# The planner's durations, hand-over times and gather latency as traced, and the slot tables built during the dense layers

## The chip, the cores and the metric

One core of a Trainium2 chip runs the program: TensorE (PE) multiplies, VectorE (DVE), ScalarE (ACT) and GpSimd (POOL) do the elementwise work, SyncE (SP) issues most DMAs. The metric is the device time of one execution in microseconds, the median of the runs shown. Each engine works through its instructions in the order in which they were emitted and waits on semaphores for the others.

## The reference, cut to what matters

```python
# attention: b=4, 8 heads, S=576, D=64
out_up    = repeat(softmax(scale * mean4(q) @ mean4(k).T) @ mean4(v), 4)      # downsampled by 4
out_local = softmax(where(|i - j| < 4, scale * q @ k.T, -1e9)) @ v            # local band
x = (out_up + out_local), as 2304 tokens x 512
# MoE 1: 8 experts, 512 -> 1024 -> 512, top 1
e_idx = argmax(x @ w_gate); gate_w = softmax(x @ w_gate)[e_idx]; eom = sigmoid(x @ w_output_gate)
out[mask_e] = gate_w * eom[:, e] * (relu(x[mask_e] @ w1[e]) @ w2[e])
# MoE 2, dense: 512 -> 2048 -> 512
h = relu(out @ w_in); result = (h * h) @ w_out
```

Everything is float32. The kernel multiplies each float32 pair as three products of rounded high and low parts (high x high, low x high, high x low).

## The kernel before, in words

Three parts follow one another on PE: attention for four batches (to about 165 us of the profile), the experts (165 to 433), the dense layers (433 to 848). The first two overlap on the other engines: weights of the first expert are split while the last batch is in attention.

**What sets the order.** No engine's order is written by hand. Class `Plan` holds operations, each with an engine, a duration in ns, a priority, what it depends on, and a ring of buffers that it takes. `Plan.order` is a greedy list scheduler over a modelled clock: it takes, again and again, the operation that could start first by that clock, and the priority breaks ties. The order in which operations are taken is the order in which they are emitted, and so the order on each engine. A duration that differs from the chip's costs nothing by itself: it moves operations in front of or behind others.

**Attention.** `reord` (L417) reorders q and k, PE transposes them, `tp_ev` (L437, ACT) evacuates them to kT and qT; `lc_k` (L584, L585, ACT) builds the block-diagonal kbd of the local band; `pd` (L508, ACT) is the exponential of the downsampled scores, `e` (L616, ACT) that of the local ones. POOL folds, VectorE does masks, maxima, sums and quotients.

**Routing and the first expert.** For the last batch the logits in PSUM (xp) go through a chain on VectorE, `mx` L696, `ex` L699, `eq` L702, `m` L705, `oh` L708, and on through counting (L713 to L828) to positions, tables of tokens and the ranking of the experts by size. The expert with most tokens of the first three batches gets a window of 256 tokens (rank -1) before the last batch is routed. Then eight windows of rank 0 to 7 follow, of 368 tokens down to 208.

**A window of an expert.** `gather` (L1121, POOL) issues an indirect DMA that fetches 128 rows of tokens into xg; `turn` (L1128, PE) transposes them into PSUM, `x_hi` (L1134, ACT) and `x_lo` (L1139, VectorE) split them into xh and xl. Weights come by DMA and are split: `w1h` L1153 and `w2h` L1160 on ACT, `w1l` L1156 on VectorE, `w2l` L1163 on POOL. Eight steps of `mm_h` (L1173, 12 matmuls into hp), `h_hi` (L1182, ACT), `h_lo` (L1187, VectorE, hl), `mm_y` (L1197, 12 matmuls into the four yp) follow; `yo` (L1204) takes the result out. The weights of the dense layers (64-bit words) are converted beside the experts (L1290 to L1301, `winl` L1216) and the early windows of the dense layers (`wol` L1391, POOL).

**The slot tables.** `compact_slots` and `overflow_slots` work out where each token's result goes, and `onehot_plan` turns slots into two tables, cid (for the main scatter, `tidc`) and oid (`tido`, for the rare tokens past a window), for each of four batches: `marks` builds a one-hot matrix oi_bm (L964), oi_a (L967) and oi_dg (L971, twice) on VectorE, `place` multiplies them on PE (L976, five short matmuls), `gather_up` adds the result (L983, L985). Some 30 us of small VectorE instructions in all. Before, cid may start when `mm_h` of rank 2 has come to its third step, oid at rank 4.

**Dense layers.** Six windows of 384 tokens, 16 steps each: `mm1` (L1347, 12 matmuls into hp, a ring of two), `relu` (L1352, ACT), `square` (L1355, VectorE, reads hp, which frees it), `s_hi` (L1359, ACT), `s_lo` (L1363, VectorE, hl), `mm2` (L1371, 9 matmuls, one step behind). At a window's end three `o_ev` and three `scatter` (POOL, indirect by tidc).

## Time and profile before

| | us |
|---|---|
| median of 3 runs | 850.5 (847.31 to 852.84) |
| profiled execution, its span | 848.5 |
| PE busy, share of the span | 786.0, 93% |
| VectorE busy, share | 497.0, 59% |
| ScalarE busy, share | 398.9, 47% |
| GpSimd busy, share | 254.8, 30% |

The profile is of one execution; 2.0 us lie between its span and the median. Busy time of PE is counted from overlapping matmuls, so 93% says where PE waits (the missing 7%), not how well it works. Shares are averages over parts with different limits: in attention ScalarE and VectorE work while PE has gaps, in the dense layers PE is never idle. The number of a line in the rows is that of the kernel before; after the change the same instruction stands one or two lines further down (L1139 becomes L1141, L964 becomes L966).

### The profile page before, as it was taken

What the parts mean: (1) busy time and instruction counts of PE and PEld (TensorE: products, weight loads), DVE (VectorE), ACT (ScalarE), POOL (GpSimd) and SP (SyncE); (2) the same over time, 40 slices, a digit from 0 to 9 for tenths busy, and PEclk for the clock granted to TensorE, in tenths of its full rate; (3) what the DMA queues carried; (4) which work ended last, traced back from release to release, by engine and by line L of the source; (5) the groups of instructions that cost most, each with busy time, mean ns of one, the idle gap of its engine ahead of it and who ended that gap; (6) DMA issues with size and microseconds to landing.
All of it is one profiled execution on the core that took longest, in us unless ns stands there. A gap on an engine that the chain in (4) does not pass through costs nothing.

```text
span 848.5 us, 15324 instructions
## 1 busy us (share of the span) xinstructions
PE 786.0 (93%) x5760; PEld 702.4 (83%) x5760; DVE 497.0 (59%) x1076; ACT 398.9 (47%) x753; POOL 254.8 (30%) x280
## 2 busy tenths in 40 slices
PE   4788998799989999898999999999999999999994
PEld 3655665598989889888998989999999999999994
DVE  6679999765547978987879973223222323322221
ACT  7998854555445456555645543223222322322221
POOL 5767543435434444445423330000001001001001
PEclk9999999899999999999999999999999999999998
DMA  8847487767467387668734332001100101001001
GB/s 224 219 112 201 131 242 221 241 221 234 153 204 231 129 256 231 178 196 258 244 121 153 120 100 68 9 1 38 38 0 38 39 1 38 1 0 38 1 1 40
DMA packets 102655, 105.39 MB, mean 124 GB/s; under 512 B 35356, under 2 KB 86556, under 8 KB 102576
## 3 DMA queue, kind: packets, MB, share of 16 engines
q1 hardware_dynamic: 99456, 94.41, 37.1%
q0 software_dynamic: 3120, 9.95, 3.4%
q8 instruction: 47, 0.77, 0.4%
q14 instruction: 32, 0.26, 0.1%
HBM read 84.95 MB, written 19.38 MB: 123 GB/s over the span
## 4 chain that ended last, share of the span: by engine, by line
PE 55%; DVE 19%; issue 10%; ACT 8%; DMA 5%; POOL 1%; SPq 0%; POOLq 0%; another core or an unknown queue 0%; ACTq 0%; DVEq 0%
PE hp L1347 18%; PE op L1371 18%; PE hp L1173 8%; PE yp L1197 8%; DMA xg<-xs_dram,idx 2%; DVE w1l L1156 2%; ACT kT L437 1%; DMA raw<-in_moe_w_in_dram 1%; ACT qT L437 1%; DVE f L1299 1%; DVE f L1301 1%; POOL w2l L1163 1%; ACT rr L417 1%; DVE f L1295 1%; DVE xT L668 1%
## 5 line engine op out<-in xcount | busy, mean ns | idle before, releaser
L1355 DVE SCALAR_TENSOR_TENSOR r<-hp,r 128x384 f32<-128x384 f32 x96 | 53.3, 555 | 191.9 <-ACT r L1352 191.9
L1352 ACT ACTIVATE r<-hp 128x384 f32<-128x384 f32 x96 | 47.1, 490 | 204.5 <-PE hp L1347 204.5
L1163 POOL TENSOR_TENSOR w2l<-r,w2h 128x512 fp32r<-128x512 f32 x72 | 101.8, 1423 | 134.6 <-ACT w2h L1160 134.1
L1347 PE MATMUL hp<-yh,winl 128*128 128x384 f32 x384 | 129.8, 338 | 0.0
L1347 PE MATMUL hp<-yh,winh 128*128 128x384 f32 x384 | 129.6, 338 | 0.0
L1347 PE MATMUL hp<-yl,winh 128*128 128x384 f32 x384 | 129.5, 337 | 0.0
L1371 PE MATMUL op<-woh,hl 128*128 128x512 f32 x288 | 113.9, 395 | 0.0
L1371 PE MATMUL op<-wol,hh 128*128 128x512 f32 x288 | 113.8, 395 | 0.1
L1381 POOL DMA_INDIRECT out_dram<-oo,tidc x18 | 17.3, 963 | 318.6 <-ACT oo L1378 315.0
L1371 PE MATMUL op<-woh,hh 128*128 128x512 f32 x288 | 112.9, 392 | 0.0
L1173 PE MATMUL hp<-xh,w1h 128*128 128x256 f32 (+7 forms) x288 | 88.6, 308 | 2.6 <-DVE hl L1187 2.6
L1173 PE MATMUL hp<-xl,w1h 128*128 128x256 f32 (+7 forms) x288 | 87.1, 302 | 0.0
L1173 PE MATMUL hp<-xh,w1l 128*128 128x256 f32 (+7 forms) x288 | 87.0, 302 | 0.0
L1197 PE MATMUL yp<-hl,w2h 128*128 128x368 f32 (+7 forms) x256 | 77.1, 301 | 3.0 <-DVE hl L1187 2.9
L1363 DVE TENSOR_TENSOR hl<-r,hh 128x384 fp32r<-128x384 f32 x96 | 53.9, 562 | 41.7 <-ACT hh L1359 41.7
L1197 PE MATMUL yp<-hh,w2h 128*128 128x368 f32 (+7 forms) x256 | 77.1, 301 | 0.9 <-DVE yo L1204 0.9
L1359 ACT ACTIVATE hh<-r 128x384 fp32r<-128x384 f32 x96 | 50.3, 524 | 54.7 <-DVE r L1355 49.7
L1197 PE MATMUL yp<-hh,w2l 128*128 128x368 f32 (+7 forms) x256 | 75.8, 296 | 0.0
L1347 PEld LDWEIGHTS hp<-yl,winh 128*128 128x128 f32 x384 | 72.3, 188 | 4.0
L1347 PEld LDWEIGHTS hp<-yh,winh 128*128 128x128 f32 x384 | 72.2, 188 | 3.7
L1347 PEld LDWEIGHTS hp<-yh,winl 128*128 128x128 f32 x384 | 72.1, 188 | 0.0
L1371 PEld LDWEIGHTS op<-woh,hl 128*128 128x128 f32 x288 | 54.1, 188 | 12.1 <-DVE hl L1363 0.3
(304 smaller groups left out, 1661.0 us busy)
## 6 DMA issues: line engine op xcount, KB each, us to landing
r<-in_moe_w_dram SPq DMA_DIRECT2D x72, 512.0 KB, 4.3
raw<-in_moe_w_in_dram SPq DMA_DIRECT2D x16, 512.0 KB, 4.7
raw<-in_moe_w_out_dram SPq DMA_DIRECT2D x16, 512.0 KB, 3.5
vbd<-in_v_dram SPq DMA_DIRECT2D x96, 64.0 KB, 3.1
yT_dram<-zero SPq DMA_DIRECT2D x8, 576.0 KB, 4.3
yr<-yT_dram SPq DMA_DIRECT2D x6, 768.0 KB, 5.2
...
```

Of the source, the lines that this page charges most:

```text
L437: self.nc.scalar.activation(dst, tp, AF.Copy)
L1156: nc.vector.tensor_tensor(W1[r, f][1], R1[r, f // 2][:, :, P * (f % 2):P * (f % 2) + P], W1[r, f][0].bitcast(F32), op=ALU.subtract)
L1163: nc.gpsimd.tensor_tensor(W2[r, f][1], R2[r, f // 2][:, f % 2, :], W2[r, f][0].bitcast(F32), op=ALU.subtract)
L1173: nc.tensor.matmul(out=ps[:, :cap], lhsT=a[:, k, :], rhs=b[:, k, :cap], start=(n == 0), stop=(n == 11))
L1197: nc.tensor.matmul(out=Y[r][c][:, :cap], lhsT=a[:, P * c:P * c + P], rhs=b[:, :cap], start=(f == 0 and n == 0), stop=(f == 7 and n == 2))
L1347: nc.tensor.matmul(out=ps[:, :WN], lhsT=a[:, k, :], rhs=b[:, k, :], start=(n == 0), stop=(n == 11))
L1352: nc.scalar.activation(r, PS[w, f][:, :WN], AF.Relu)
L1355: nc.vector.scalar_tensor_tensor(SQ[w, f], PS[w, f][:, :WN], 0.0, SQ[w, f], op0=ALU.max, op1=ALU.mult)
L1359: nc.scalar.activation(SQ[w, f, 1][0], SQ[w, f], AF.Copy)
L1363: nc.vector.tensor_tensor(sl, SQ[w, f], sh.bitcast(F32), op=ALU.subtract)
L1371: nc.tensor.matmul(out=O[w][t], lhsT=a[:, P * t:P * t + P], rhs=b, start=(f == 0 and n == 0), stop=(f == 15 and n == 2))
L1381: ins = nc.gpsimd.indirect_dma_start(out=self.out, out_offset=bass.IndirectOffsetOnAxis(ap=self.tidc[:, 3 * w + t:3 * w + t + 1], axis=0), ...
```

## The change

Three things, none of which changes what is computed. First, `Plan.order`'s model: a hand-over between engines was 230 ns for all, and is now 260 after PE, 150 after ACT, 125 after VectorE, 110 after POOL, 230 after SP, 40 more when POOL receives, 120 (was 130) on one engine; a DMA occupies the modelled queue 1.2 times as long. Second, durations in the model: `tp_ev` 490 to 880 and 270 to 310, `fold_end` 940 to 1500, `lc_k` 1520 to 1780, `lc_s` 1600 to 1400, `pv_mm` 1010 to 1090, `reord` 900 to 950, `mm_h` and `mm_y` from 5 ns a token and 20 to 5.43 ns a token, a gather 1050 to 1270 with its latency from 1900 to 4500, `x_hi` somewhat less, `w1_hi` and `w2_hi` 500 to 530, `w2_lo` 1220 to 1420, the conversions 500 to 575, 520 to 540 and 1240 to 1420, `mm1` 1930 to 2110, `mm2` 1930 to 2090, `scatter` 1050 to 1270. Third, the tables: cid depends on the first `mm1` of dense window 1, oid on that of window 2, both at a late priority; `place` takes its PSUM buffer from the ring of `mm1` (hp); the dense layers' pools (`sw2`) no longer wait for the tables. Docstrings go. The core of the diff:

```diff
@@ Plan.order
-        ops, gives, hop = self.ops, self.gives, 230
+        ops, gives = self.ops, self.gives
+        after = dict(PE=260, ACT=150, DVE=125, POOL=110, SP=230)
+        hop = lambda a, b: after.get(a, 230) + (40 if b == "POOL" else 0)
...
-                        early[o] = max([0] + [end[x] + (hop if ops[x]["eng"] != d["eng"] else 0 if d["eng"] in ("PE", "SP") else 130) if ops[x]["eng"] else start[x] for x in d["deps"]])
+                        early[o] = max([0] + [end[x] + (hop(ops[x]["eng"], d["eng"]) if ops[x]["eng"] != d["eng"] else 0 if d["eng"] in ("PE", "SP") else 120) if ops[x]["eng"] else start[x] for x in d["deps"]])
...
-                dma_free = max(dma_free, t + d["dur"]) + d["dma"]
+                dma_free = max(dma_free, t + d["dur"]) + 1.2 * d["dma"]
@@ onehot_plan
-            U["ps"] = self.qx.tile([P, 4, P], F32, name="xp").rearrange("p a b -> p (a b)")[:, 0:2 * ncol]
+            U["ps"] = self.qh.tile([P, 512], F32, name="hp")[:, 0:2 * ncol]
...
-            op(nm + "_p", (b,), "PE", 120, prio - 40, place, [(nm + "_m", b)], take="qx")
+            op(nm + "_p", (b,), "PE", 150, prio - 40, place, [(nm + "_m", b)], take="qh")
...
@@ moe1_plan
-            mm = 12 * cap / 2.4 + 20
+            mm = 12 * max(118, 0.4525 * cap)
...
-                op("gather", (r, k), "POOL", 1050, at(-5, -3), gather, early + [("fa_i",) if first else ("fr_i", min(r, 1))] + rows(r),
-                   lat=1900, dma=600, take="xg")
+                op("gather", (r, k), "POOL", 1270, at(-5, -3), gather, early + [("fa_i",) if first else ("fr_i", min(r, 1))] + rows(r),
+                   lat=4500, dma=600, take="xg")
...
-        op("cmp", (), "DVE", [80, 230, 230, 230, 230, 100, 100, 100, 100, 150], 60, self.compact_slots, [("sw1",), ("fr_o",), ("mm_h", 2, 2)])
-        self.onehot_plan("cid", lambda: self.cp, 18, lambda: self.tidc, 60, [("cmp",)])
-        op("ovs", (), "DVE", [240] * 24, 61, self.overflow_slots, [("cid_f",), ("mm_h", 4, 2)])
-        self.onehot_plan("oid", lambda: self.ov, NOV, lambda: self.tido, 61, [("ovs",)])
+        op("cmp", (), "DVE", [80, 230, 230, 230, 230, 100, 100, 100, 100, 150], 118, self.compact_slots, [("sw2",), ("fr_o",), ("mm1", 1, 0)])
+        self.onehot_plan("cid", lambda: self.cp, 18, lambda: self.tidc, 118, [("cmp",)])
+        op("ovs", (), "DVE", [240] * 24, 150, self.overflow_slots, [("cid_f",), ("mm1", 2, 0)])
+        self.onehot_plan("oid", lambda: self.ov, NOV, lambda: self.tido, 150, [("ovs",)])
@@ moe2_plan
-        op("sw2", (), None, 0, 200, moe2_pools, [o for o in one if o[0] in ("mm_h", "mm_y", "y_out", "y_st", "x_hi", "x_lo", "cid_p", "cid_f", "oid_p", "oid_f")] + [("sw2a",)])
+        op("sw2", (), None, 0, 200, moe2_pools, [o for o in one if o[0] in ("mm_h", "mm_y", "y_out", "y_st", "x_hi", "x_lo")] + [("sw2a",)])
...
-                op("mm1", (w, f), "PE", 1930, t, mm1, [("cxi", f)] + [("y_lo", w, k) for k in range(4)], take="qh")
+                op("mm1", (w, f), "PE", 2110, t, mm1, [("cxi", f)] + [("y_lo", w, k) for k in range(4)], take="qh")
```

Where it moves instructions, as the order of emission shows. PE, window of rank 1, before: the first `turn` (xp<-ident,xg) of rank 1 stands inside rank 0's window, behind 48 `mm_h` and the first 12 `mm_y` matmuls of rank 0 (yp; the x behind a row counts matmuls).

```order
L1197 MATMUL yp_3427<-hh,w2h 128x368
L1197 MATMUL yp_3427<-hl,w2h 128x368
L1197 MATMUL yp_3427<-hh,w2l 128x368
L1128 MATMUL xp<-ident,xg 128x128 x4
L1197 MATMUL yp_3424<-hh,w2h 128x368
```

PE, the same place after the change:

```order
L1199 MATMUL yp_3427<-hh,w2h 128x368
L1199 MATMUL yp_3427<-hl,w2h 128x368
L1199 MATMUL yp_3427<-hh,w2l 128x368
L1130 MATMUL xp<-ident,xg 128x128 x8
L1175 MATMUL hp<-xh,w1h 128x368
```

The turn stands behind the first 24 `mm_y` matmuls instead of 12, and its two full chunks are together. The first turn of rank 2 moves by 12 matmuls likewise, and its gather on POOL stands behind six w2l since rank 1's gathers, where it stood behind seven. The first turns of ranks 5 and 7 stand behind 36 `mm_y` matmuls of the window that runs, instead of 24; that of rank 4 keeps its place.

VectorE, the end of the last batch's routing, before (w1l: weights of the first expert; mx to oh: the routing chain; xl: the first expert's tokens, low part):

```order
L668 TENSOR_TENSOR xT<-tx,dso 128x4x96
L1156 TENSOR_TENSOR w1l<-r_2647,w1h 128x512 x2
L696 TENSOR_REDUCE mx<-xp 128x5
L699 TENSOR_TENSOR ex<-xp,mx 128x40
L702 SCALAR_TENSOR_TENSOR eq<-ex,w_87 128x40
L1139 TENSOR_TENSOR xl<-hp,xh 128x4x128
L705 TENSOR_REDUCE m_2811<-eq 128x5
L708 SCALAR_TENSOR_TENSOR oh<-m_2811,eq 128x40
L1139 TENSOR_TENSOR xl<-hp,xh 128x4x128
L831 TENSOR_TENSOR ot<-oh,tokhl 128x80
```

VectorE, the same place after the change, and further down the two xl:

```order
L670 TENSOR_TENSOR xT<-tx,dso 128x4x96
L1158 TENSOR_TENSOR w1l<-r_2641,w1h 128x512
L698 TENSOR_REDUCE mx<-xp 128x5
L701 TENSOR_TENSOR ex<-xp,mx 128x40
L704 SCALAR_TENSOR_TENSOR eq<-ex,w_87 128x40
L707 TENSOR_REDUCE m_2776<-eq 128x5
L710 SCALAR_TENSOR_TENSOR oh<-m_2776,eq 128x40
L833 TENSOR_TENSOR ot<-oh,tokhl 128x80
```

```order
L907 TENSOR_REDUCE offe<-gn 128x8
L828 TENSOR_TENSOR tok<-th,xp 128x40
L1141 TENSOR_TENSOR xl<-hp,xh 128x4x128
L924 TENSOR_TENSOR tokr<-tok 128x24
L909 TENSOR_TENSOR offe<-offe,ca 128x8
L926 TENSOR_TENSOR tokr<-tokr,ra 128x24
L911 TENSOR_TENSOR gn<-ro,offe 128x64
L928 TENSOR_TENSOR tokr<-tokr,tok 128x24
L915 TENSOR_REDUCE offi<-gn 128x8
L1141 TENSOR_TENSOR xl<-hp,xh 128x4x128
```

One w1l has gone from in front of the chain, and both xl have moved from within it to behind the routing's tables (30 and 37 rows after oh). On POOL in the same place five w2l in a row were emitted behind the two gathers of the first expert; after the change one w2l stands ahead of the gathers, then one w2l, xo, two w2l. On PE the second `turn` of the first expert now stands behind the five matmuls L820 (th, of the routing).

VectorE, the first table (cid), before, in the expert layer:

```order
L958 CAST oi_pf<-oi_pi 128x40
L964 TENSOR_TENSOR oi_bm<-iob,oi_pf 128x640
L1139 TENSOR_TENSOR xl<-xp,xh 128x4x32
L967 TENSOR_TENSOR oi_a_4351<-iob,oi_pf 128x90
L971 TENSOR_TENSOR oi_dg<-oi_a_4351,tokhl 128x5x18 x2
L1187 SCALAR_TENSOR_TENSOR hl<-hp,hh 128x312
L1156 TENSOR_TENSOR w1l<-r_4214,w1h 128x512
L983 COPY oi_acc<-xp 128x36
```

VectorE, the first table after the change, in window 1 of the dense layers (r: square, hl: s_lo):

```order
L1357 SCALAR_TENSOR_TENSOR r<-hp,r 128x384
L960 CAST oi_pf<-oi_pi 128x40
L966 TENSOR_TENSOR oi_bm<-iob,oi_pf 128x640
L1365 TENSOR_TENSOR hl<-r,hh 128x384
L969 TENSOR_TENSOR oi_a_7168<-iob,oi_pf 128x90
L973 TENSOR_TENSOR oi_dg<-oi_a_7168,tokhl 128x5x18 x2
L985 COPY oi_acc<-hp 128x36
L966 TENSOR_TENSOR oi_bm<-iob,oi_pf 128x640
L1357 SCALAR_TENSOR_TENSOR r<-hp,r 128x384
L969 TENSOR_TENSOR oi_a_7208<-iob,oi_pf 128x90
L973 TENSOR_TENSOR oi_dg<-oi_a_7208,tokhl 128x5x18 x2
```

The table's instructions of one batch stand between `square` and `s_lo` of a dense step instead of between `h_lo` and `w1l`; on PE the five matmuls of `place` stand between an `mm1` and an `mm2`, four times in window 1 and four times in window 2, and no longer between `mm_h` and `mm_y`.

## Rows read from the trace of the kernel before

**Rows 1.** Windows: stretch, length, busy of PE PEld DVE ACT POOL, clock, DMA.

```profile
18.50:40.00 21.50, 16.42 (x268) 13.01 (x272) 14.39 (x32) 21.36 (x29) 14.16 (x24) 1.00 0.78 199
...
165.40:433.00 267.60, 248.65 (x1851) 243.04 (x1848) 199.35 (x400) 143.66 (x287) 120.26 (x90) 0.98 0.66 208
...
466.00:836.00 370.00, 369.93 (x1848) 334.24 (x1847) 131.97 (x233) 110.06 (x219) 27.65 (x25) 1.00 0.09 31
```

**Rows 2.** Waits of PE in the expert layer, 165 to 433: total, times, longest.

```profile
PE xp L1128 <- DMA xg<-xs_dram,idx: 8.2, 6, 2.5
PE xp L976 <- DVE oi_dg L971: 4.3, 4, 1.4
PE xp L713 <- DVE oh L708: 3.7, 1, 3.7
PE yp L1197 <- DVE hl L1187: 2.9, 5, 1.2
PE hp L1173 <- DVE hl L1187: 2.6, 1, 2.6
```

**Rows 3.** Windows with PE's granted clock behind three stalls, columns as in rows 1.

```profile
165.40:171.20 5.80, 5.80 (x32) 5.63 (x29) 4.73 (x22) 1.86 (x5) 1.59 (x1) 0.50 0.87 311
...
236.70:239.90 3.20, 3.20 (x14) 3.20 (x13) 1.98 (x3) 0.60 (x1) 0.00 (x0) 0.55 0.63 186
...
359.50:363.70 4.20, 4.18 (x24) 4.18 (x24) 3.13 (x8) 0.63 (x1) 0.00 (x0) 0.65 0.92 194
```

**Rows 4.** Timeline before the first expert: start, duration, instruction, idle before.

```profile
157.59 6.07 DVE L1156 TENSOR_TENSOR w1l<-r,w1h 128x512 fp32r<-128x512 f32 x2 [0.43 <-ACT w1h L1153]
157.72 5.39 POOL L1163 TENSOR_TENSOR w2l<-r,w2h 128x512 fp32r<-128x512 f32 x4
...
165.23 0.19 PE L713 MATMUL xp<-oh,tri 128*128 128x40 bf16 x1 [3.71 <-DVE oh L708]
```

**Rows 5.** Timeline of VectorE behind oh, columns as in rows 4.

```profile
165.84 0.19 DVE L723 TENSOR_TENSOR zs<-xp,oh 128x40 f32<-128x40 f32 x1
...
167.23 0.82 DVE L806 TENSOR_TENSOR bm<-iob,pi 128x640 bf16<-128x640 f32 x1
167.96 1.26 DVE L773 TENSOR_SCALAR xo<-xo,s 128x512 f32<-128x512 f32 x1
...
169.57 0.56 DVE L813 TENSOR_TENSOR dg<-k,ot 128x400 bf16<-128x400 f32 x1
```

**Rows 6.** DMA issues of the page: gathers, count, median us to landing.

```profile
xg<-xs_dram,idx POOLq DMA_INDIRECT x21, 6.5
```

**Rows 7.** Instructions of VectorE by line, 260 to 390: count, busy, mean.

```profile
L1156 DVE TENSOR_TENSOR w1l<-r,w1h 128x512 fp32r<-128x512 f32 x35 | 25.0, 715 | 2.4 <-ACT w1h L1153 2.0
...
L964 DVE TENSOR_TENSOR oi_bm<-iob,oi_pf 128x640 bf16<-128x640 f32 x8 | 7.6, 955 | 0.1
...
L967 DVE TENSOR_TENSOR oi_a<-iob,oi_pf 128x90 f32<-128x90 f32 (+1 forms) x8 | 6.3, 792 | 0.0
```

**Rows 8.** Timeline at a stall of PE behind the second table.

```profile
359.05 0.42 DVE L1187 SCALAR_TENSOR_TENSOR hl<-hp,hh 128x256 fp32r<-128x256 f32 x1
...
359.52 0.58 PE L1173 MATMUL hp<-xh,w1h 128*128 128x256 f32 x1 [2.56 <-DVE hl L1187]
```

**Rows 9.** Timeline at a place of the first table, POOL idle since 281.88.

```profile
283.11 0.24 DVE L967 TENSOR_TENSOR oi_a<-iob,oi_pf 128x90 f32<-128x90 f32 x1
```

**Rows 10.** Instructions of ScalarE by line, 18.5 to 60.

```profile
L437 ACT ACTIVATE qT<-tp 128x512 f32<-128x512 f32 (+1 forms) x12 | 11.1, 1002 | 0.1
...
L616 ACT ACTIVATE e<-e 128x512 f32<-128x512 f32 x4 | 2.6, 658 | 0.0
```

**Rows 11.** Timeline of a dense step; its matmuls in the chain.

```profile
512.22 0.56 DVE L1363 TENSOR_TENSOR hl<-r,hh 128x384 fp32r<-128x384 f32 x1 [0.59 <-ACT hh L1359]
...
512.60 2.11 PE hp L1347 x12
514.71 2.09 PE op L1371 x9
```

More of the change, by code (lines that the diff above doesn't have):

```diff
@@ L109, in order @@
                     if len(hs) >= self.rings[d["take"]]:
-                        after = gives[hs[-self.rings[d["take"]]]]
-                        if any(x not in end for x in after):
+                        freed = gives[hs[-self.rings[d["take"]]]]
+                        if any(x not in end for x in freed):
                             continue
-                        t = max([t] + [end[x] + hop for x in after])
+                        t = max([t] + [end[x] + hop(ops[x]["eng"], d["eng"]) for x in freed])
                 c = (t, d["prio"], o)
@@ L283, in plan_b @@
             for i in range(2):
-                op("reord", (b, nm, i), "ACT", 900, tau - 0.2, self.reord, [("load", b, nm, i)], take="rr")
+                op("reord", (b, nm, i), "ACT", 950, tau - 0.2, self.reord, [("load", b, nm, i)], take="rr")
                 self.plan.give("raw", ("load", b, nm, i), ("reord", b, nm, i))
@@ L330, in plan_b @@
             i = (b, t3)
-            op("lc_k", i, "ACT", 1520, k - 0.2, self.lc_k, [("tp_ev", b, "k", t) for t in range(4 + (t3 == 2))], take="kbd")
-            op("lc_s", i, "PE", 1600, k, self.lc_s, [("lc_k",) + i] + [("tp_ev", b, "q", t) for t in range(4 + (t3 == 2))], take="psc")
+            op("lc_k", i, "ACT", 1780, k - 0.2, self.lc_k, [("tp_ev", b, "k", t) for t in range(4 + (t3 == 2))], take="kbd")
+            op("lc_s", i, "PE", 1400, k, self.lc_s, [("lc_k",) + i] + [("tp_ev", b, "q", t) for t in range(4 + (t3 == 2))], take="psc")
             self.plan.give("kbd", ("lc_k",) + i, ("lc_s",) + i)
@@ L1230, in plan_moe1 @@
                 n = min(P, cap - P * k)
-                op("gather", (r, k), "POOL", 1050, at(-5, -3), gather, early + [("fa_i",) if first else ("fr_i", min(r, 1))] + rows(r),
-                   lat=1900, dma=600, take="xg")
+                op("gather", (r, k), "POOL", 1270, at(-5, -3), gather, early + [("fa_i",) if first else ("fr_i", min(r, 1))] + rows(r),
+                   lat=4500, dma=600, take="xg")
                 op("turn", (r, k), "PE", 440, at(0, -6), turn, [("gather", r, k)], take="qh" if first else "qx")
                 give("xg", ("gather", r, k), ("turn", r, k))
-                op("x_hi", (r, k), "ACT", 3.8 * n + 20, at(0, -6), x_hi, [("turn", r, k)], take="x" if k == 0 else None)
+                op("x_hi", (r, k), "ACT", 3.55 * n + 30, at(0, -6), x_hi, [("turn", r, k)], take="x" if k == 0 else None)
                 op("x_lo", (r, k), "DVE", 4.2 * n + 70, at(0, -6), x_lo, [("x_hi", r, k)])
@@ L1243, in plan_moe1 @@
                 for f in (2 * s, 2 * s + 1):
[L1244 removed]
+                    op("w1_hi", (r, f), "ACT", 530, at(f, f - 4), w1_hi, [("load1", r, s)], take="w1")
                     op("w1_lo", (r, f), "DVE", 600, at(f, f - 3.5), w1_lo, [("w1_hi", r, f)])
[L1246 to L1247 removed]
+                    op("w2_hi", (r, f), "ACT", 530, at(f + 5, f - 3.9), w2_hi, [("load2", r, s)], take="w2")
+                    op("w2_lo", (r, f), "POOL", 1420, at(f + 5, f - 3.4), w2_lo, [("w2_hi", r, f)])
                     give("w1", ("w1_hi", r, f), ("mm_h", r, f))
@@ L1394, in plan_moe2 @@
         for f in range(16):
-            self.conv_plan("o", f, tau - 4 + 2 * f, [("sw2a",) if f < 5 else ("sw2",)], wo_hi, wo_lo, "POOL", 1240)
+            self.conv_plan("o", f, tau - 4 + 2 * f, [("sw2a",) if f < 5 else ("sw2",)], wo_hi, wo_lo, "POOL", 1420)
         for w in range(6):
@@ L1414, in plan_moe2 @@
                 give("rr2", ("relu", w, f), ("s_lo", w, f))
-                op("mm2", (w, f), "PE", 1930, t + 1, mm2, [("s_lo", w, f), ("cxo", f), ("sw2",), ("mm2", w, f - 1)], take="qo" if f == 0 else None)
+                op("mm2", (w, f), "PE", 2090, t + 1, mm2, [("s_lo", w, f), ("cxo", f), ("sw2",), ("mm2", w, f - 1)], take="qo" if f == 0 else None)
                 give("h", ("s_hi", w, f), ("mm2", w, f))
@@ L1418, in plan_moe2 @@
                 op("o_ev", (w, t), ("ACT", "DVE")[t % 2], 600, tau + 32, o_ev, [("mm2", w, 15)], take="oo")
-                op("scatter", (w, t), "POOL", 1050, tau + 32, scatter, [("o_ev", w, t), ("cid_f",), ("zero_y", 0)], lat=2200, dma=750)
+                op("scatter", (w, t), "POOL", 1270, tau + 32, scatter, [("o_ev", w, t), ("cid_f",), ("zero_y", 0)], lat=2200, dma=750)
                 give("oo", ("o_ev", w, t), ("scatter", w, t))
```

15 lines of the change are left out of this document (6 added, 9 removed).

## The prediction

> **What bounds the kernel now.** I read the windows first, then the waits of TensorE in the expert layer, then the timeline round each wait, and last the chain in a dense step.
>
> The windows split the span in three. In the dense layers PE is busy for 369.93 of 370.00 us [rows 1]: nothing to win there, only to lose. In the expert layer it is busy for 248.65 of 267.60 us, so 18.95 us are stalls. Attention is the third part: ScalarE is busy for 21.36 of 21.50 us from 18.5 to 40 us, VectorE for 14.39 only, which is to say that VectorE is fed late by ScalarE.
>
> The waits say what the stalls of the expert layer are [rows 2]: PE waits 8.2 us in 6 turns for a gather to land; 4.3 us in 4 places for a slot table (oi_dg); 2.9 and 2.6 us for hl, the low part that VectorE makes. The 3.7 us for oh lie just ahead of the first expert. The 2.6 us for hl belong to the second table too: its oi_bm and the rest stand in front of that hl on VectorE, and the first mm_h of the next step starts when it is done [rows 8].
>
> After a stall the clock counts again. Behind the waits at 236.0 and 359.5 the granted clock is 0.55 for 3.20 us and 0.65 for 4.20 us; behind the 3.7 us before the first expert it is 0.50 for 5.80 us [rows 3]. At the full clock the work of such a stretch would take its length times the clock, so these cost 3.20 x 0.45 = 1.4, 4.20 x 0.35 = 1.5 and 5.80 x 0.5 = 2.9 us.
>
> **The change, part by part.** The sum is made against the profiled execution's span, 848.5 us; the median of the runs shown is 2.0 us above it, and I add that at the end.
>
> *Gathers.* The model had a gather land 2.95 us after its issue began (1050 + 1900 ns); the median on the chip is 6.5 us [rows 6]. So turns were placed where the gather could not have landed. The new numbers make 5.77 us. The order shows the result: the first turns of ranks 1, 2, 3, 5 and 7 stand 12 matmuls, about 2 us, later behind the same gather, and rank 2's gather leaves POOL one w2l earlier. The longest wait was 2.5 us; 5 of the 6 waits should go, or nearly. What stays is 6.5 - 5.8 = 0.7 us at one or two of them, and rank 4, whose turn keeps its place. I take -7.2 of the 8.2.
>
> *Tables out of the expert layer.* The 4.3 us for oi_dg go with the five matmuls that waited. Of the 5.5 us for hl I take -4: the 2.6 are behind table work by the row [rows 8], and two of the shorter ones stand among the table's instructions. The matmuls of place move and cost as much there as here, so they are nil in the sum. Of the slow stretches behind stalls, 1.4 + 1.5 = -2.9. VectorE, no longer carrying some 30 us of table work between 268 and 385, must still serve w1l, hl, xl and the conversions; another order on all engines will put some new waits between 0 and 8 us there. I take +3, about what the hl and yo waits without tables and gathers come to now, and keep 0 and 8 as the ends.
>
> Expert layer: -7.2 - 4.3 - 4 - 2.9 + 3 = -15.4.
>
> *Start of the first expert.* Two w1l took 6.07 us on VectorE while four w2l ran on POOL for 5.39 us [rows 4]; a w1l takes 0.715 us on the mean [rows 7]. The new order has one w1l less in front of the chain of the last batch's routing, and on POOL a w2l, two gathers, a w2l and xo instead of five w2l in a row. Where two w1l took 6.07 us one will take 0.7, so oh should come some 5 us earlier, at 160.2 instead of 165.2. But the first expert does not start then. Its two xl have moved behind the routing's tables, and on PE its second turn stands behind th (L820), which needs bm and dg. From zs to bm 15 small instructions start in 1.4 us, 0.1 us each; bm takes 0.82, xo 1.26, dg 0.56 [rows 5]. To dg it is some 20 x 0.1 + 2 x 0.7 (w1l) + 0.8 + 1.2 + 0.6 = 6.0 us; then th 0.7, the turn 0.65, two hand-overs and x_hi some 1.0: 8.4 us. So the first mm_h starts near 168.6 instead of 165.4: **+3.2**, between 0 (if the instructions fit into waits) and +6 (if POOL still holds VectorE up, below). The stretch at clock 0.50 behind it stays, since PE still idles before it.
>
> *Tables in the dense layers.* A dense step takes 2.11 + 2.09 = 4.2 us of PE, and hl is done at 512.22 + 0.56 = 512.78, while the mm2 that needs it starts at 514.71: 1.9 us of slack [rows 11]. On VectorE a step needs two instructions of 0.56, 1.1 of 4.2 us, and the table adds up to one oi_bm, one oi_a and two oi_dg: by the rows of the expert layer some 0.95 + 0.8 + 0.7 = 2.4 us in each of 8 steps [rows 7], and less with POOL idle, where an oi_a took 0.24 us [rows 9]. In sum VectorE has 3.5 of 4.2 us to do. At worst all 2.4 us stand in the way of a step's square and hl, less what VectorE would have waited for s_hi anyway: hl is then 0.5 us past its slack. oi_bm in front of square also holds the hp of an mm1 longer, whose ring has two. I take **+0.5**, between 0 and +4 (8 steps late by 0.5).
>
> *Attention.* The order of ScalarE has two qT, a pair of kbd and two e fewer in front of the first exponential of batch 0's downsampled part. With 0.66 us for e and 1.0 for qT [rows 10] those six are 4 to 6 us that VectorE and PE get their first work earlier. But total work is unchanged, and what is put off comes later; VectorE's idle time from 18.5 to 40 is 21.5 - 14.39 = 7.1 us, the most that this could give. I take **-3**, between -8 and +4 (the same six instructions late where they matter).
>
> *Durations without a place of their own* (mm_h, mm1, conversions, scatter) only make the model's PE slower and nearer to the chip; POOL has 27.65 us of work in 370 [rows 1], so the scatter's is nothing. Where they shift something it is in the +3.
>
> Sum: -3 + 3.2 - 15.4 + 0.5 = -14.7, so a span of 833.8, and with the 2.0 us above it **836 us**.
>
> **The rivals.**
>
> *New waits eat the gain.* A list scheduler's order is brittle: the waits in the expert layer now come from five sources, and taking two away lets the next come up. For it: VectorE is busy for 199 of 267.6 us there [rows 1], 30 of it table work. Against: what is taken away is the longest of the waits, and 12 matmuls later is the direct answer to each. If new waits are 9 instead of 3 us, the time is 842; with attention at 0 as well, 845.
>
> *POOL holds VectorE up.* The row shows it now: w1l at 3.0 instead of 0.7 us beside w2l [rows 4]. If the w2l that stay in the new order fall on the routing chain, each instruction caught can lose most of a w2l, 5.39 / 4 = 1.35 us; two of them make the first expert start at +6 instead of +3.2: 839. [...]
>
> *Slower: the dense steps lose.* If the table work puts hl past its 1.9 us of slack, PE stalls in each step that carries it, and a stalled PE's clock falls besides. Some 14 steps carry table work. To end 1% above the median, 859, each would have to lose (859 - 836) / 14 = 1.6 us, that is hl 3.5 us late. For it: VectorE at 3.5 of 4.2 us. Against: 2.4 us of extra work a step cannot be 3.5 us late unless it runs longer than in the expert layer. The same side has attention at +4 and the first expert at +6 with no gain at the hl waits.
>
> *The moved tables do nothing.* The waits for oi_dg would be taken by hl waits; the gathers alone give -7.2 and the clock -1.4. With the other waits as they are, -3 + 3.2 - 7.2 - 1.4 + 0.5 = -7.9: 843.
>
> **How the numbers follow.** My forecast, all waits down to about a fifth: 0.57, with its own range 829 to 842. New waits eat the gain, or the tables give nothing (842 to 849): 0.25. POOL holds up VectorE (839, within the first range): counted in the 0.57. Attention and first expert both good, below 829: 0.10. Slower by the dense steps or attention: 0.08. The range 824 to 849 leaves out the last and some of the lowest. A change of about 1% is what a measurement of this kernel can tell from none: below 842 0.70, 842 to 859 0.22, above 859 0.08.
>
> **What would show it.** In the waits of PE in the expert layer the rows for xg and oi_dg gone or below 1.5 us together, and hl below 3. The windows: the expert layer 252 us long instead of 267.6, with PE above 97%. The first mm_h at 168 to 169 if attention gave nothing, 165 to 166 if it gave 3, behind an oh that is 5 us earlier. In the dense layers PE still above 99.5% busy, its steps in windows 1 and 2 at 4.2 to 4.4 us. Wrong if the first mm_h comes after 172, if new waits for w1l, w2l or yo sum to more than 5 us, or if PE waits for square or hl in the dense windows 1 and 2.

## The result: 1.0% slower, and the profile after

The changed kernel takes 856.9 us (855.4 to 858.1) against 849.3 us: ratio 1.0102, 95% interval 1.0059 to 1.0144. 836 was forecast, so the direction was wrong too. The profiled execution has a span of 855.8 us, 7.3 above that of before.

The windows of after, cut where its parts meet (stretch, length, busy of PE PEld DVE ACT POOL, clock, DMA), to be read beside [rows 1]:

```profile
18.50:40.00 21.50, 16.98 (x267) 13.15 (x267) 16.35 (x42) 20.44 (x28) 16.46 (x27) 1.00 0.85 210
...
166.80:175.50 8.70, 2.02 (x13) 1.31 (x11) 8.63 (x30) 2.41 (x4) 3.79 (x4) 0.50 0.77 246
175.50:433.00 257.50, 246.98 (x1812) 241.32 (x1813) 166.97 (x273) 142.11 (x284) 115.92 (x90) 0.98 0.66 211
433.00:466.00 33.00, 31.77 (x159) 27.62 (x158) 29.40 (x51) 17.68 (x36) 8.27 (x6) 1.00 0.47 149
466.00:843.30 377.30, 374.38 (x1898) 336.13 (x1897) 153.12 (x328) 110.24 (x221) 26.53 (x24) 1.00 0.09 29
```

VectorE does get its work earlier (16.35 instead of 14.39 us busy from 18.5 to 40). The expert layer is 10 us shorter, 257.5 instead of 267.6. But it begins 10 us later, at 175.5 instead of 165.4, after 8.7 us in which PE hardly works. And the dense layers, which had PE busy without a break, now have gaps.

PE's waits after, of three stretches (140 to 175, 175 to 433, 433 to the end), to be read beside [rows 2]:

```profile
PE xp L820 <- DVE dg L815: 6.0, 1, 6.0
PE hp L1130 <- DMA xg<-xs_dram,idxa: 2.3, 1, 2.3
...
PE xp L715 <- DVE oh L710: 0.8, 1, 0.8
```

```profile
PE yp L1199 <- DVE hl L1189: 2.9, 6, 0.8
PE xp L1130 <- DVE xl L1141: 2.2, 1, 2.2
PE yp L1199 <- ACT yo L1208: 2.0, 1, 2.0
PE yp L1199 <- ACT hh L1184: 1.0, 2, 0.6
PE xp L1130 <- DMA xg<-xs_dram,idx: 0.7, 2, 0.5
```

```profile
PE op L1373 <- DVE hl L1365: 2.3, 4, 1.3
PE op L1373 <- ACT hh L1361: 1.8, 4, 0.8
```

In the expert layer the waits for gathers (8.2 to 0.7) and for oi_dg (4.3 to none) are gone as forecast; waits for xl and hh are new, and that for yo is 2.0 instead of 0.9 us. The 3.7 us for oh have become 6.0 us for dg. The dense layers had no wait at all before; the 4.1 us here all lie in window 0, where no table work is.

Where the 7.3 us are, from five places of the two timelines (the start of the last xT and of oh on VectorE, the first mm_h, the first mm1, the end of PE's last matmul):

| | before | after | difference |
|---|---|---|---|
| last xT | 156.60 | 160.21 | +3.6 |
| last xT to oh | 8.38 | 3.18 | -5.2 |
| oh to first mm_h | 0.42 | 12.08 | +11.7 |
| expert layer, first mm_h to first mm1 | 267.68 | 257.61 | -10.1 |
| dense layers, first mm1 to end of PE | 404.74 | 411.46 | +6.7 |
| behind PE's end | 10.67 | 11.22 | +0.6 |

### The profile page after: what moved, and what is told of

It reads as the page before. It is cut to its first block, busy times and chain, and to the rows that moved or that the text cites. A ratio compares the mean times of both kernels' runs of the same rounds, so it can differ in the third digit from the quotient of the medians.

```text
span 855.8 us, 15327 instructions
## 1 busy us (share of the span) xinstructions
PE 794.0 (93%) x5760; PEld 702.2 (82%) x5760; DVE 490.9 (57%) x1076; ACT 399.5 (47%) x753; POOL 250.4 (29%) x280
## 4 chain that ended last, share of the span: by engine, by line
PE 59%; DVE 16%; issue 10%; ACT 7%; DMA 6%; POOL 1%; SPq 0%; POOLq 0%; another core or an unknown queue 0%; ACTq 0%; DVEq 0%
PE hp L1349 18%; PE op L1373 17%; PE yp L1199 10%; PE hp L1175 8%; DVE f L1301 2%; DVE f L1297 2%; DMA xg<-xs_dram,idx 2%; DMA raw<-in_moe_w_in_dram 1%; DVE f L1303 1%; PE tp L755 1%; DVE f L1299 1%; ACT rr L419 1%; PE po L650 1%; ACT f L1292 1%; ACT kT L439 1%
## 5 line engine op out<-in xcount | busy, mean ns | idle before, releaser
L1165 POOL TENSOR_TENSOR w2l<-r,w2h 128x512 fp32r<-128x512 f32 x72 | 99.0, 1380 | 145.9 <-ACT w2h L1162 145.0
L1175 PE MATMUL hp<-xh,w1h 128*128 128x256 f32 (+7 forms) x288 | 86.7, 301 | 1.3 <-ACT xh L1136 0.7
```

The lines of the kernel that those rows point to most:

```text
L1165: nc.gpsimd.tensor_tensor(W2[r, f][1], R2[r, f // 2][:, f % 2, :], W2[r, f][0].bitcast(F32), op=ALU.subtract)
L1175: nc.tensor.matmul(out=ps[:, :cap], lhsT=a[:, k, :], rhs=b[:, k, :cap], start=(n == 0), stop=(n == 11))
```

## The experiments

The change was taken apart. T is the third part (tables); H the hand-over times with the DMA factor; A the durations of attention; G gather; M mm_h, mm_y and the splits; D conversions, dense matmuls and scatter. Each run is the kernel before with the named parts, if nothing else is said. A ratio is against the kernel before on the same chip, whose median was 847.7 to 849.4 us there, so ratios are compared and not the times. Times of places are of the one profiled execution.

| run | parts | us | ratio, 95% interval | xT | oh | mm_h | expert | dense |
|---|---|---|---|---|---|---|---|---|
| before | | 849.3 | | 156.6 | 165.0 | 165.4 | 267.7 | 404.7 |
| after | all | 856.9 | 1.010 (1.006 to 1.014) | 160.2 | 163.4 | 175.5 | 257.6 | 411.5 |
| e1 | T | 839.5 | 0.988 (0.984 to 0.991) | 157.1 | 165.5 | 165.9 | 256.4 | 406.8 |
| e1b | T again | 841.4 | 0.990 (0.987 to 0.994) | 158.2 | 166.4 | 166.8 | 254.2 | 406.8 |
| e2 | HAGMD | 866.2 | 1.020 (1.018 to 1.023) | 161.8 | 164.9 | 177.0 | 269.9 | 409.7 |
| e3 | GMDT | 853.5 | 1.005 (1.003 to 1.007) | 157.5 | 165.7 | 168.2 | 261.7 | 412.4 |
| e4 | GMT | 852.5 | 1.004 (1.001 to 1.006) | 157.7 | 165.9 | 168.5 | 264.2 | 409.7 |
| e5 | T, G of ranks 0 to 7 | 842.0 | 0.992 (0.989 to 0.995) | 157.3 | 165.2 | 165.6 | 254.7 | 406.8 |
| e6 | TA | 844.8 | 0.995 (0.992 to 0.998) | 166.9 | 172.3 | 168.2 | 256.4 | 406.8 |
| e7 | TH | 854.5 | 1.007 (1.004 to 1.011) | 163.8 | 167.8 | 180.8 | 250.6 | 406.7 |
| e8 | TD | 847.9 | 0.999 (0.997 to 1.002) | 158.4 | 165.6 | 166.3 | 253.2 | 412.8 |
| e9 | T, mm1 and mm2 of D | 848.7 | 0.998 (0.996 to 1.001) | 158.1 | 166.0 | 166.4 | 255.7 | 413.4 |
| e10 | after, lag two | 857.0 | 1.007 (1.004 to 1.010) | 161.3 | 164.5 | 176.6 | 256.2 | 412.2 |
| e11 | after, w2l later | 857.3 | 1.008 (1.006 to 1.011) | 160.0 | 163.2 | 174.3 | 258.7 | 411.6 |
| e12 | T, w2l later | 842.4 | 0.991 (0.987 to 0.994) | 156.3 | 163.2 | 163.6 | 260.2 | 406.8 |
| e13 | after, lag two on | 853.7 | 1.008 (1.005 to 1.011) | 157.1 | 160.2 | 172.3 | 258.9 | 408.5 |
| e14 | after, wait filled | 854.5 | 1.009 (1.006 to 1.012) | 159.2 | 162.4 | 174.0 | 254.8 | 411.9 |
| e15 | T, H in ranks 0 to 7 without the DMA factor | 841.1 | 0.991 (0.987 to 0.994) | 158.4 | 166.7 | 167.1 | 253.4 | 408.5 |

By their ratios e10, e11, e13 and e14 cannot be told from after; what they show is read from their stages. The dense layers repeat best: 406.7 to 406.8 us in six profiles (e1, e1b, e5, e6, e7, e12).

**The two halves (e1, e2).** e1 has the hunks of `onehot_plan`, of the four lines of cmp, cid, ovs, oid and of `sw2`, and no other; e2 has all the others:

```diff
# e1, e2 without it
+        op("cmp", (), "DVE", [...], 118, self.compact_slots, [("sw2",), ("fr_o",), ("mm1", 1, 0)])
# e2, e1 without it
+        after = dict(PE=260, ACT=150, DVE=125, POOL=110, SP=230)
```

> The planner's numbers as before, only the slot tables moved into the dense layers. Theory A (the tables are the good part, and cost only their place in the dense steps): first expert matmul at 165.4 as before, the expert layer some 9 us shorter (the 4.3 us for oi_dg, about 3 to 4 us of hl waits and 1.5 us of low clock gone), each of 8 dense steps longer by 0.22 us as in the changed kernel, 1.8 us: a span of about 841, ratio 0.992. Theory B (the tables are what makes the dense layers lose, by 6.7 us): the expert layer 9 us shorter, dense layers 6.7 us longer, 846, ratio 0.997. Theory C (new waits take the place of those for the tables): 848 to 851.

> All new numbers in the planner (hand-over times, durations, gather latency), the tables where they were, in the expert layer. Theory A (the numbers lose 10 us before the first expert and 5 us in dense window 0, and win 7 to 8 us at the gathers): first expert matmul at 174 to 176, the table waits of 4 us or more still there, dense layers 4 to 5 us longer, a span of 855 to 862. Theory B (the dense loss is the tables'): dense layers as before, 850 to 854.

The tables alone make the kernel 1.2% faster, the numbers alone 2.0% slower: the change is two changes of opposite sign. e1 is theory A, with an expert layer shorter by 11.3 us, 2 more than expected. Its windows of the expert and the dense layers, and what is left of PE's waits in the first:

```profile
165.90:422.30 256.40, 245.49 (x1812) 241.89 (x1809) 167.84 (x304) 143.69 (x287) 116.19 (x90) 0.98 0.68 218
422.30:829.00 406.70, 406.54 (x2070) 366.26 (x2068) 184.26 (x380) 128.93 (x256) 38.31 (x32) 1.00 0.12 41
```

```profile
PE xp L1128 <- DMA xg<-xs_dram,idx: 6.7, 5, 2.1
PE xp L713 <- DVE oh L708: 3.7, 1, 3.7
PE yp L1197 <- DVE hl L1187: 2.2, 4, 0.8
PE yp L1197 <- DVE yo L1204: 1.8, 1, 1.8
```

oi_dg is gone, hl is down from 5.5 to 2.2 us, VectorE from 199 to 168 us busy. Some 2.3 us of the 11.3 are the 40 matmuls of `place`, which left the expert layer; before, they had PE busy there for 2.34 us (the window of the expert layer with L976 alone: PE, PEld):

```profile
165.40:433.00 267.60, 2.34 (x40) 1.69 (x40) 0.98 0.66 208
```

The dense layers take all the table work at PE 406.54 of 406.70. They are 2.0 us longer for it, without a wait: the chain of after shows how (start, duration, piece; place stands between hp and op, and a step takes 4.43 instead of 4.20 us, in 8 steps 1.8).

```profile
513.35 2.11 PE hp L1349 x12
515.59 2.19 PE op L1373 x9
517.78 2.11 PE hp L1349 x12
```

e2 is worse than both theories; its table waits stay (3.3 us), hl costs 6.9, and its dense layers are 5 us longer without any table in them, so that loss is the numbers'.

**Which numbers (e3 to e8).** Each is the kernel before with the named hunks of the diff:

```diff
# e3, e4, e8: D in e3 and e8, not in e4
+                op("mm1", (w, f), "PE", 2110, ...)
# e3, e4 for all ranks, e5 for ranks 0 to 7
+                op("gather", (r, k), "POOL", 1050 if first else 1270, ..., lat=1900 if first else 4500, ...)
# e6
+                op("tp_ev", (b, nm, t), "ACT", 880 if big else 310, ...)
# e7
+        hop = lambda a, b: after.get(a, 230) + (40 if b == "POOL" else 0)
```

> The change without the new hand-over times, DMA factor and attention durations: ScalarE's order in attention is that of before. Theory A (these numbers made attention later by 3.6 us and put both xl of the first expert behind the routing's tables): oh at 165.2 as before, first expert matmul at 165 to 168, expert layer as in the changed kernel (257 to 260 us), dense layers 5 to 7 us longer than before: 845 to 849. Theory B (the new gather latency alone moves the xl and the turns of the first expert): first expert matmul at 172 or later, 852 or more.

> Only the new gather latency, the new numbers of the expert layer and the moved tables; hand-over, attention, conversion and dense durations as before. Theory A (the 4 to 5 us lost in dense window 0 come from the new durations of conversions and dense matmuls): dense layers only 1.8 us longer than before, no wait of TensorE for hl or hh in dense window 0, a span some 4 us below that of the run with those numbers: 841 to 844. Theory B (what is left in window 0 depends on when the experts end, not on these numbers): dense layers 5 to 7 us longer here too, 845 to 849.

> The moved tables with the planner's other numbers as before, and the new gather duration and latency for ranks 0 to 7 (not for the first expert's two gathers). Against the run with only the tables moved (839.5, expert layer 256.4 us, 6.7 us of waits for gathers). Theory A (the gather numbers are worth their waits, as the prediction had it): waits for gathers down to 1 us or less, expert layer 250 to 252, dense layers as there, 834 to 836. Theory B (turns that are put later only hand their waits on to hl, hh, xl or yo): expert layer 255 to 259, the waits under other names, 839 to 843.

> The moved tables, and only the new durations of attention (kT and qT evacuation, fold_end, kbd, local scores, probabilities times v, reordering). Theory A (these durations make attention late): last transposed tokens (xT) at 160 us or later instead of 157.1, oh 3 us later or more, 842 to 847. Theory B (attention is lost by the new hand-over times, not by these): xT at 155 to 158; both xl now stand ahead of the last routing chain, so that the first expert can start before oh: first expert matmul at 160 to 165, 834 to 840.

> The moved tables, and only the new hand-over times between engines with the DMA factor 1.2. Theory A (hand-over times are what puts both xl and the turns of the first expert behind the routing's tables): first expert matmul 8 to 12 us after oh, at 173 to 178, expert and dense layers not better than with the tables alone: 847 to 853. Theory B (the attention durations do that): first expert matmul within 3 us of oh, 838 to 843.

> The moved tables, and only the new durations of the conversions, of the dense matmuls and of the scatter. Theory A (the 5 us of dense window 0 are these durations' doing): attention and first expert as with the tables alone, TensorE waits for square, hh or hl in dense window 0 again, 3 to 5 us, dense layers 409 to 412 instead of 406.7, 843 to 846. Theory B (window 0's waits come from how the expert layer ends): dense layers 406 to 408, 838 to 841.

e3 and e4 have attention as before (xT 157.5), and start the first expert 2.6 us after oh instead of 0.4: G and M have a part in that delay, the rest is elsewhere. The time of e3 is in theory B's range, but not by its late start (168.2, not 172); e4 was slower than either theory had it. Both have expert layers of 262 and 264 us and dense layers of 412 and 410. With 4.9 us more than before in the dense layers, and 2.3 us of waits for square, hl and hh there, e4 is near theory B: window 0 also loses without D. Why their expert layers are 5 and 8 us longer than that of e1 was not tested: e5 clears G in ranks 0 to 7, and no run has M alone. e7 is theory A at the start: with the hand-over times and the DMA factor the first mm_h comes 12.9 us behind oh, and xT comes 6.7 us later than in e1. e6 is theory A for xT, 9.8 us later than in e1, but its xl stand ahead of the last routing chain, so that the first expert starts 4 us before oh, and of the 10 us only 2 remain. e8 is theory A: dense layers 6.1 us longer by the numbers of D.

e5 is theory B. The gathers' waits fell from 6.7 to 0.9 us, and others came in their place, as the waits of its expert layer show:

```profile
PE yp L1197 <- ACT yo L1206: 2.8, 2, 2.6
PE yp L1197 <- DVE hl L1187: 2.6, 6, 0.8
PE xp L1128 <- DVE xl L1139: 2.4, 2, 1.7
...
PE xp L1128 <- DMA xg<-xs_dram,idx: 0.9, 2, 0.6
```

Its expert layer of 254.7 us is between the 256.4 and 254.2 of the two profiles of e1: the gather numbers gave nothing beyond the 2.1 us by which these two differ.

**Dense window 0 (e9, e10, e13).** In the order of before and of e1, e5, e6 and e7, mm2 runs two to four steps behind mm1 in dense window 0 (48 mm1 matmuls, 18 mm2, then 24 and 18 in turn); in after, e2, e8 and e9 it runs one to two behind after the first few steps (12 and 9 in turn), and so it does in e4, which has none of D. The kernels of the first kind have no wait for square, hh or hl there, all those of the second have. A longer lag is not better by itself: e3 takes three steps at a time (36 and 27 in turn) and waits 4.1 us for square and 1.5 us for hl.

```diff
# e9: the kernel before, with T and
+                op("mm1", (w, f), "PE", 2110, ...)
+                op("mm2", (w, f), "PE", 2090, ...)
# e10: after, with this on the dependencies of mm2
+ ([("mm1", 0, f + 2)] if w == 0 and f < 14 else [])
# e13: after, with this
+ ([("mm1", 0, f + 2) if f < 14 else ("mm1", 1, f - 14)] if w == 0 else [])
```

> The moved tables, and of the planner's numbers only the two of the dense matmuls (mm1 1930 to 2110, mm2 1930 to 2090). By the order mm2 then runs one step behind mm1 in dense window 0, where before, and with the tables alone, it runs two steps behind. Theory A (these two numbers alone turn the order of window 0, and one step of lag is too little beside the conversions): waits of TensorE for hl, hh or wol in window 0, dense layers 410 to 413 instead of 406.7. Theory B (the conversions' durations do it): dense layers 406 to 408, no such waits.

> The changed kernel, with mm2 of dense window 0 made to depend on the mm1 two steps on, so that it runs two steps behind as before the change. Theory A (the lag is what costs the dense layers 4 to 5 us): start and expert layer as in the changed kernel, first dense matmul near 433, no waits in window 0, dense layers 406.5 to 408.5 instead of 411.5: 852 to 854. Theory B (VectorE has too much to do in window 0 whatever the lag): dense layers 410 to 412, 855 to 858.

> The changed kernel, with mm2 of dense window 0 made to depend on the mm1 two steps on, over the window's end too (the last two of window 0 on the first two mm1 of window 1). Theory A (one step of lag is too little beside the conversions, two are enough): no or nearly no waits in the first 45 us of the dense layers, dense layers 406.5 to 409 instead of 411.5, 852 to 854. Theory B (the backlog on VectorE in window 0 is the same whatever the lag, and is paid later): dense layers 410.5 to 412.5, with the waits at the end of window 0, 855 to 858.

e9: theory A; two numbers are enough for 6.7 us beyond e1. They are not needed for it, as e4 shows. Its waits in the dense layers, and those of e13:

```profile
PE op L1371 <- DVE hl L1363: 2.6, 7, 0.6
PE op L1371 <- ACT hh L1359: 1.6, 3, 0.9
```

```profile
PE hp L1349 <- DVE r L1357: 1.1, 1, 1.1
PE op L1373 <- DVE hl L1365: 0.9, 3, 0.4
PE hp L1349 <- DVE oi_acc L987: 0.3, 1, 0.3
```

e10 came out on theory B's side, 412.2, but for a reason of its edit: its steps were all 2.07 to 2.11 us for the first 40 us, where after loses some 5 up to 482, and most of the loss came at the window's end, where the dependency stopped and the order emptied its backlog. e13 carries it over that end: 408.5 instead of 411.5, theory A, with 2.3 us of waits left, all behind the first 40 us. Why the lag matters is on VectorE: beside square (r) and s_lo (hl) it has the four instructions of a conversion to do in each step of window 0 (a stretch of after; L1303 is the fourth):

```profile
442.60 0.42 DVE L1297 TENSOR_SCALAR f<-f 128x512 f32<-128x512 f32 x1
442.93 0.55 DVE L1365 TENSOR_TENSOR hl<-r,hh 128x384 fp32r<-128x384 f32 x1
443.40 0.42 DVE L1299 TENSOR_SCALAR f<-f 128x512 int32<-128x512 int32 x1
443.86 1.67 DVE L1301 SCALAR_TENSOR_TENSOR f<-raw,f 128x512 int32<-128x512 int32 x1
```

The planner has 335, 335, 602 and 602 ns for these, 1.9 us in sum; that L1301 took 1.67 us, and on the mean the four take 2.8 us in window 0 of after (0.57, 0.52, 1.04 and 0.69). With 0.55 for square and 0.67 for s_lo VectorE has some 4.0 us to do in a step of 4.2. Before it had as much (2.9, 0.55 and 0.59), and PE had no wait at the longer lag. Why the numbers turn the order is my reading of the planner, and not shown: with mm1 at 1930 its PE was faster than its VectorE and put mm1 ahead; with the true 2110 it believed PE to be the slower one, and left mm2 one step behind a VectorE that is in truth slower than it thinks. The order of e4, where mm1 is at 1930, came about some other way.

**The first expert (e11, e12).** Plan dependencies that move w2l of the first expert later on POOL; they move the emission only, and POOL does not wait on the chip.

```diff
# e11: after; e12: the kernel before with T, and rt_g1 in place of rt_tk
-  w2_lo, [("w2_hi", r, f)])
+  w2_lo, [("w2_hi", r, f)] + ([("rt_tk", NB - 1)] if first else []))
```

> The changed kernel, with the first expert's w2l on GpSimd held until the last batch's routing has its positions (th). xl still stands behind the routing's tables. Theory A (GpSimd's w2l stretches the routing's instructions on VectorE, by 1.6, 1.1 and 1.1 us in the changed kernel): sm, pi and bm back at 0.2, 0.2 and 0.8 us, oh to the first expert matmul 8 to 9 us instead of 12.1, first expert matmul near 172. Theory B (the long instructions come from elsewhere): oh to first expert matmul 11 to 13 us, 174 to 176.

> The moved tables with all the planner's numbers as before, and the first expert's w2l on GpSimd held until the last batch's oh is there; VectorE's order before oh is that of before. Theory A (four w2l on GpSimd stretch two w1l to 6.1 us): these two back at 1.4 us, oh at 160 to 162 instead of 165.5, first expert matmul at 161 to 163, expert layer 256 to 258: 834 to 837. Theory B (w1l is slow for another reason, such as the weights' arrival): oh at 165, no gain, 839 to 842; or the held w2l come too late for mm_y of the first expert and TensorE waits for them: above 840.

The timeline of after between oh and the first expert:

```profile
163.39 0.20 DVE L710 SCALAR_TENSOR_TENSOR oh<-m,eq 128x40 bf16<-128x40 f32 x1
...
165.14 1.83 DVE L741 TENSOR_SCALAR sm<-sm 128x5 f32<-128x5 f32 x1
...
165.65 1.28 POOL L1165 TENSOR_TENSOR w2l<-r,w2h 128x512 fp32r<-128x512 f32 x1
...
169.12 2.67 POOL L1165 TENSOR_TENSOR w2l<-r,w2h 128x512 fp32r<-128x512 f32 x2
...
169.37 1.23 DVE L805 TENSOR_SCALAR pi<-posi 128x5 int32<-128x5 int32 x1
...
170.58 1.89 DVE L808 TENSOR_TENSOR bm<-iob,pi 128x640 bf16<-128x640 f32 x1
...
173.40 0.49 PE L820 MATMUL xp<-dg,bm 128*128 128x80 bf16 x5 [6.00 <-DVE dg L815]
...
175.47 0.58 PE L1175 MATMUL hp<-xh,w1h 128*128 128x256 f32 x1 [0.69 <-ACT xh L1136]
```

and of e11:

```profile
164.90 0.16 DVE L741 TENSOR_SCALAR sm<-sm 128x5 f32<-128x5 f32 x1
...
167.52 5.50 POOL L1165 TENSOR_TENSOR w2l<-r,w2h 128x512 fp32r<-128x512 f32 x4
...
167.57 1.89 DVE L808 TENSOR_TENSOR bm<-iob,pi 128x640 bf16<-128x640 f32 x1
...
169.38 1.28 DVE L884 TENSOR_TENSOR G<-n 128x64 f32<-128x64 f32 x1
...
171.90 1.56 DVE L815 TENSOR_TENSOR dg<-k,ot 128x400 bf16<-128x400 f32 x1
```

In after three instructions of VectorE (sm, pi, bm) take 1.83, 1.23 and 1.89 us beside w2l on POOL, where before bm took 0.82 [rows 5] and sm and pi 0.16 each:

```profile
166.26 0.16 DVE L739 TENSOR_SCALAR sm<-sm 128x5 f32<-128x5 f32 x1
...
167.01 0.16 DVE L803 TENSOR_SCALAR pi<-posi 128x5 int32<-128x5 int32 x1
```

That is 3.8 us more in all. (sm began 0.5 us ahead of its w2l, while POOL issued a gather.) In e11 the w2l run 2 us later and sm is back at 0.16, but pi is still at 1.01, beside POOL's xo, and bm at 1.89, and G, k and dg are long as well (1.28, 1.26, 1.56). So the stretching follows the work of POOL, but e11 did not get rid of it, and its total says nothing (theory B's 11.2 us from oh to mm_h, by theory A's mechanism). e12 is the cleaner one:

```profile
157.33 3.77 DVE L1156 TENSOR_TENSOR w1l<-r,w1h 128x512 fp32r<-128x512 f32 x2 [0.43 <-ACT w1h L1153]
```

With two w2l beside them instead of four the two w1l took 3.77 us instead of 6.07, and oh came at 163.2 instead of 165.5. Its time is theory B's all the same: the expert layer was 4 us longer, by waits of 14.8 instead of 10.9 us, and nothing was won.

**Attention's clock (e14).** 12 more matmuls ahead of the product with vd in the last batch, where after waits 1.73 us for vd:

```diff
+            if b == NB - 1 and hf == 0 and c == 0:
+                for _ in range(12):
+                    nc.tensor.matmul(out=po[0:HD, 288:288 + SD], lhsT=vd[:, 0, :], rhs=pts[:, pr, 0, :], start=True, stop=True, ...)
```

> The changed kernel with 12 more matmuls (128x64 by 144, into a part of the PSUM tile that nothing reads) ahead of the product with vd in the last batch, in the place where TensorE waited 1.73 us for vd. They add work and leave the result as it is. Theory A (that idle stretch is what the granted clock falls behind, and the low clock is what makes attention late): clock 1.00 from 139 to 150 instead of 0.50 to 0.63, last transposed tokens (xT) at 156 to 157.5 instead of 160.2, oh at 160 to 161, first expert matmul at 171.5 to 173: 851 to 854. Theory B (the clock falls for another reason, such as little work in the stretch as a whole): clock 0.5 again, xT at 160 or later, 856 to 858.

Windows at that place, of after, e14 and e13 (columns as above):

```profile
136.00:139.00 3.00, 1.27 (x16) 0.59 (x10) 2.94 (x14) 1.03 (x3) 0.06 (x1) 1.00 0.91 258
139.00:145.00 6.00, 6.00 (x33) 3.88 (x34) 4.50 (x22) 1.99 (x5) 0.99 (x1) 0.54 0.86 261
145.00:150.00 5.00, 5.00 (x35) 3.29 (x36) 1.54 (x8) 2.38 (x4) 0.00 (x0) 0.53 0.30 111
```

```profile
139.00:145.00 6.00, 6.00 (x55) 4.95 (x54) 5.67 (x29) 2.21 (x6) 1.05 (x1) 1.00 0.90 258
```

```profile
139.00:145.00 6.00, 5.13 (x42) 3.62 (x42) 5.80 (x30) 2.75 (x7) 1.05 (x1) 1.00 0.98 286
```

With the wait filled the clock stays at 1.00, as theory A had it. Its xT of 159.2 does not show the gain, because the run ended the batch before 2.4 us later than after did. e13 gives the size without having been made for it: its attention is that of after, with the same wait of 1.7 us, but there the clock did not fall. So the length of the last batch is the measure, from the last xT of the batch before to the last xT of all: 24.1 us in e13 and 25.2 in e14, with its added matmuls; 27.1 to 28.7 in after, e2, e10 and e11, where the clock fell; 22.6 in before. The fall costs 3 to 4.6 us, and the order itself 1.5. The wait alone does not fix the fall: one of five executions with it stayed at 1.00, and so the one of e14 does not prove that the filling kept it there.

**A better version? (e15, e1b).**

```diff
# the kernel before with T, and the new hand-over times where the receiver is an operation of ranks 0 to 7
+        hop = lambda a, b, o: after.get(a, 230) + (40 if b == "POOL" else 0) if new(o) else 230
```

> The moved tables; the new hand-over times only where the receiving operation belongs to the expert layer of ranks 0 to 7 (gather, turn, splits, mm_h, mm_y, taking out). Attention, the first expert and the order of dense window 0 are those of the run with the tables alone. Theory A (nearer hand-over times make the expert layer's order better, and only their effect on attention and the first expert lost): first expert matmul at 165 to 167, expert layer 249 to 253, dense layers 406 to 407: a span of 832 to 836. Theory B (the short expert layer in the run with all hand-over times came of its other start, with weights further ahead): expert layer 254 to 259, 838 to 842.

> The kernel with only the tables moved, once more on this chip: 838 to 841, ratio 0.985 to 0.992, expert layer 255 to 258. If its expert layer differs by more than 2 us from the 256.4 of its first profile, differences of that size between the runs say nothing.

The expert layer of e15 lies between the theories (253.4 us, beside 254.2 for e1b on the same chip), its dense layers are 1.7 us longer, with 1.1 us of waits for wol, and the time is theory B's, that of e1b. The short expert layer of e7 (250.6) did not come with the hand-over times in the expert layer. No kernel here is measurably faster than the tables alone, twice about 1% below before.

## Why the prediction was wrong, step by step

Between the forecast (-14.7) and the result (+7.3) lie 22.0 us: attention 6.6, the start of the first expert 3.3, the expert layer 5.3, the dense layers 6.2, behind PE's end 0.6. Of the three signs of being wrong one came, the first mm_h after 172 (175.5). The chances do not quite add up either: 0.57 and 0.10 make 0.67 below 842, where 0.70 stands.

**Tables out of the expert layer: right.** -4.3 - 4 - 1.5 was forecast for oi_dg, hl and the clock behind them, and +0.5 for the dense layers, with `place` nil in the sum: -9.3. e1 gave -11.3 and +2.0 with nothing else changed, -9.3 too; `place` with its 2.3 us is in both. That the sum meets to the tenth is luck, as e1b gave -13.4 and +2.0.

**Gathers: the waits right, the gain wrong.** The waits fell as forecast (8.2 to 0.7), but the -7.2 us were not to be had: in e5 the expert layer stayed where it was, the stall renamed to yo, hl and xl. The step that failed is that I let new waits cost a fixed +3. In sum -15.4 was forecast for the expert layer, -10.1 came, and the tables alone give as much. My rival of new waits was the true one for this term.

**Start of the first expert: the mechanism right, mis-sized.** oh was forecast 5 us nearer to xT, and came 5.2 nearer. From oh to the first mm_h 8.4 us were forecast and 12.1 came: 10.0 instead of 6.0 to the end of dg, and 2.1 instead of 2.4 behind it. The difference is, by the rows, the 3.8 us of stretched routing instructions, the rival that I priced at 2.8 and left out of the sum. Two of the six stretched instructions in after and e11 (sm, pi) are TENSOR_SCALAR, with a single tensor to read, and took 1.83 and 1.23 us instead of 0.16; by what GpSimd holds them up no run shows.

**Attention: wrong sign.** -3 was forecast, +3.6 came. VectorE's earlier start was seen (16.35 instead of 14.39 us busy), and at the end of the second batch xT was 6.2 us ahead (103.0 instead of 109.2); but at the end of the third 2.4 us were left (131.6 instead of 134.0), and the last batch took 28.7 instead of 22.6. Of these 6.1 us 4.6 are the granted clock at 0.54 behind a wait of 1.73 us, by the 24.1 of e13, where the clock did not fall; there xT came at 157.05, 0.4 after that of before, so that the early work bought nothing at the end even so. The step that failed is in the clock and in the order of the last batch: I had counted the clock behind the waits that went, and none behind waits that come.

**Dense layers: the step that failed outright.** The tables gave +2.0 (e1), without a wait, as said. But the change gave +6.7, and the larger part is dense window 0, of which I said that durations without a place of their own are in the +3. I priced a dense step from window 1, where mm2 is one step behind mm1 in both kernels, and did not look at the order of window 0, where it showed plainly: 24 and 18 matmuls in turn before, 12 and 9 after. e9 shows that the two durations of mm1 and mm2 alone do it, e4 that the other numbers can do it too, and e13 that two steps of lag give 3.0 us of it back.

My rival of slower dense steps put the loss on the table work in windows 1 and 2, and there was no wait there; the dense layers did lose, in window 0 and by the planner's numbers. The clock, which I let fall behind each such stall, stayed at 1.00 in window 0, behind waits of up to 1.3 us (447 to 505 in after).

What stays open: why attention loses most of its lead in the third batch, when the clock falls behind a wait and when not (same order, same wait, both seen), and what M does by itself. A start of the first expert with no w2l on POOL was not reached by either edit.
